# Moving the second mixture's small tiles in SBUF and adding two gaps between its tile pools

## The chip, the cores and the metric

The kernel runs on one core of a Trainium2 chip. The metric is the device time of one execution in microseconds; the time before is the median of 3 runs, 1181.48 us (1179.54 to 1184.17).

## The reference

An attention layer with a recurrent memory feeds a soft mixture of experts, and its result feeds a second mixture in which every expert sees every token and the shares P are balanced by eight rounds of row and column sums:

```python
def _moe2_ref(x, w_gate, w1, w2):
    N, D, E, F = (2304, 512, 8, 1024)
    P = np.exp(x @ w_gate - (x @ w_gate).max())
    for _ in range(8):
        P /= P.sum(1, keepdims=True) + 1e-09
        P /= P.sum(0, keepdims=True) + 1e-09
        P *= N / E
    out = np.zeros((N, D), dtype=np.float32)
    for e in range(E):
        h = np.maximum(x @ w1[e], 0.0)
        out += P[:, e:e + 1] * (h @ w2[e])
    return out
```

All inputs and outputs are float32.

## The kernel before, in words

The attention and the first mixture fill the first part of the program. The change touches only the second mixture, which works on 8 experts e times 9 units u of 256 tokens (72 units g in that order).

For each unit, `layer1` (L1030) makes the hidden layer: 8 matmuls `l`, each with a 128x128 piece of `a4s[e]` as the stationary operand and 256 columns of `c4T` as the moving one. ScalarE, VectorE and GpSimd (`hidden`, L1079) turn that into the tiles a11, a12, a22, s1, s2, s3, s4, each split into a high part h and a low part l of 2048 bytes per partition (four 128x128 stationary pieces); a21 of the first units shares its tile with s3. The second layer is a seven-product scheme: `product` (L1344) runs the products in the order p5, p1, p7, p6, p2, p3, p4, which pairs s1 with T1, a11 with B11, s3 with T3, s2 with T2, a12 with B21, s4 with B22 and a22 with T4. One product is 12 matmuls: for each of four pieces f, h against the weights' h (L1354), h against l (L1355) and l against h (L1356). The h and l tiles are stationary, and 256 columns of the weight tile W are moving. B11 and T3 lie in `BB1`, and B21 and B22 in `BB2`. After the second product, `layer1` of the next unit is put in. The first 6 units use `plain` (L1316) instead, with 48 matmuls of 512 moving columns. `collect` (L1359) adds each product onto the accumulators in VectorE. The order of TensorE, VectorE, ScalarE and GpSimd is written out by hand in this part (L1410 on); what stands outside that block, the writing of `sel` (L972, L978) among it, is placed by the scheduler as its operands and its space come free.

Places in SBUF. A pool's tiles lie one after another in the order in which they are first asked for, each rounded up to 32 bytes (buffers of one tag lie together), and the pools mA, mB, mC, mD follow each other in the order in which they are opened. The pools reuse space of the first mixture; with `reuse_waits="tile"` the first writer of a tile waits for the last user of whatever lay in that tile's own space. The first bytes of the tiles, by 512, are:

| tiles | pool | bytes per partition | start by 512 |
|---|---|---|---|
| c4T (moving in `layer1`) | cst | 9728 | 416 |
| T1, T2 of even experts, BB1 | mA | 4096, 8192 each | 416 |
| accA, accB, accD | mB | 18432, 18432, 9216 | 416 |
| Pr | mB | 576 | 416 |
| soB/c4, ahi, alo, a11, a21/s3, a12, a22, ft | mB | multiples of 512 | 480 |
| rr, cs | mB | 72, 32 | 480, 64 |
| cP, chi, f (3 buffers), s1, s2, s4 | mB | multiples of 512 | 96 |
| T1, T2 of odd experts, raw, BB2, T4 | mC | multiples of 512 | 96 |
| sel, Cw, gsel, m1, m2 | mD | 2560, 2304, 160, 4, 4 | 96, 96, 352, 0, 32 |
| a4 (2 buffers, stationary in `layer1`) | mD | 4096 each | 64 |

The 512 bytes are the length of one stationary piece (128 float32). The steps f go by 512 bytes in the hidden tiles, by 1024 or 2048 in the weights, and by 1024 per unit in c4T, so one residue holds for every matmul of a pair. In mD, `sel` lies on the bytes on which the first mixture keeps both of its `hT` tiles (L820), which its last matmuls (L848) read.

At the start of the second mixture VectorE copies `soT` (L858), writes `sel` (L972 once, L978 three times), copies `soB` four times (L1120) and makes `alo` (L1003); TensorE multiplies `ahi` and `alo` with `sel` (L1017, L1018) into the first `a4`, from which the first `layer1` runs.

Of the kernel before, what the change touches and what calls it, by code (L numbers as in the profile page):

```python
# [8 lines left out]
F32 = mybir.dt.float32  # L9
BF16 = mybir.dt.bfloat16  # L10
F32R = mybir.dt.float32r
# [10 lines left out]
def infini_attention_soft_moe_sinkhorn_moe(  # L22
# [18 lines left out]
    E = moe2_w1.shape[0]  # L41
    FF = moe2_w1.shape[1] * moe2_w1.shape[4]
    NS = moe_phi.shape[2]
    SPE = NS // E
    P = 128
# [8 lines left out]
    NTT = N // P  # L54
# [706 lines left out]
    with bctx:  # L761
# [57 lines left out]
        for g in range(E // 4):  # L819
# [3 lines left out]
            for n in range(FF // 512):  # L823
# [3 lines left out]
                for c in range(KD):  # L827
                    for j in range(4):
                        e = SPE * (4 * g + j)
# [41 lines left out]

    mA = ctx.enter_context(tc.tile_pool(name="mA", bufs=1, reuse_waits="tile"))
    mB = ctx.enter_context(tc.tile_pool(name="mB", bufs=1, reuse_waits="tile"))
    mC = ctx.enter_context(tc.tile_pool(name="mC", bufs=1, reuse_waits="tile"))
    mD = ctx.enter_context(tc.tile_pool(name="mD", bufs=1, reuse_waits="tile"))
    ps_l = ctx.enter_context(tc.tile_pool(name="ps_l", bufs=1, space=PSUM, reuse_waits="tile"))
# [91 lines left out]
        )  # L968


    sel = mD.tile([P, 4, 160], F32R, name="sel")
    nc.vector.tensor_scalar(  # L972
        out=sel.rearrange("p j c -> p (j c)"), in0=ones[:, 0:1].to_broadcast([P, 640]),
# [2 lines left out]
    for r in (0, 2, 4):  # L976
# [1 line left out]
        nc.vector.tensor_copy(  # L978
            sel[:, :, 32 * r : 32 * r + 32], ident.rearrange("p (j s) -> p j s", j=4)
        )  # L980
    a2s, a4s, G = {}, {}, {}

    def aux(nm):
        return ps_a.tile([P, 512], F32, tag="a", name=nm)
# [13 lines left out]
    def split_a(e):  # L998
        pa = a2s[e]
        ahi = mB.tile([P, 256], F32R, tag="ahi", name="ahi")  # L1000
        nc.scalar.activation(out=ahi, in_=pa[:, 0:256], func=AF.Copy)
        alo = mB.tile([P, 256], F32R, tag="alo", name="alo")
        nc.vector.tensor_tensor(  # L1003
            out=alo, in0=pa[:, 0:256], in1=ahi.bitcast(F32), op=ALU.subtract
        )
        a2s[e] = ahi, alo
        a4s[e] = mD.tile([P, FF], F32R, tag="a4", name="a4", bufs=2)

    def spread_a(e, n):

# [97 lines left out]

    soR = soT.rearrange("p c (o s) -> p c o s", o=1)
    Pr = mB.tile([P, NTT, E], F32, name="Pr")  # L1110
    Cw = mD.tile([P, NTT, NS], F32, name="Cw")

    gsel = mD.tile([P, E + NS], F32R, name="gsel")
    m1 = mD.tile([P, 1], F32, name="m1")
    m2 = mD.tile([1, 1], F32, name="m2")

    def gate_slots():
        soB = G["soB"] = mB.tile([P, KD, 4, NS], F32, tag="c4", name="soB")
# [51 lines left out]
        nc.scalar.activation(out=Pr, in_=Pr, func=AF.Exp, bias=m1)  # L1170

    def balance_rows():
        rr = mB.tile([P, NTT], F32, tag="rr", name="rr")
        nc.vector.tensor_reduce(out=rr, in_=Pr, op=ALU.add, axis=AX.X)
        nc.vector.tensor_scalar_add(rr, rr, 1e-9)
        nc.vector.reciprocal(rr, rr)
        nc.vector.tensor_tensor(
            out=Pr, in0=Pr, in1=rr.rearrange("p (t o) -> p t o", o=1).to_broadcast([P, NTT, E]),
            op=ALU.mult,
        )  # L1180
        cs = G["cs"] = mB.tile([P, E], F32, tag="cs", name="cs")
        nc.vector.tensor_reduce(
            out=cs, in_=Pr.rearrange("p t e -> p e t"), op=ALU.add, axis=AX.X
        )
# [56 lines left out]
    for n in range(8):  # L1241
        beside(9 + 3 * n, balance_rows)
        beside(10 + 3 * n, sum_columns)
        beside(11 + 3 * n, balance_columns)
# [43 lines left out]
    for e in range(1, E):  # L1288
        v = NU * (e - 1)
        for i in range(5):  # L1290
            c_steps(v + 6 + i, e, 2 * i, min(2 * i + 2, NU))
        at(v, 0, load_w1, e, e % 2)
        at(v + 3 * (e == 1), 4, load_raw, e)
        at(v + 1, 3, prepare_a, e)
        at(v + 1, 4, split_a, e)
        for n in range(2):
            at(v + 1, 5 + 2 * n, spread_a, e, n)
            at(v + 1, 6 + 2 * n, store_a, e, n)
        for i in range(2):
            for n, nm in enumerate(("T1", "T2", "T4")):  # L1300

                s = 29 + 4 * (3 * i + n) if e == 1 else 7 * (v + 2 + 3 * i + n) + 1
                beside(s, w_sum, e, nm, i, "P")
                beside(s + 2 - (e == 1), w_hi, e, nm, i)
                beside(s + 3 - (e == 1), w_lo, e, nm, i, "P")
            at(v + 6 + i, 2, w_sum, e, "T3", i, "P")
        for nm, k in (("B11", 2), ("T3", 4), ("B21", 6), ("B22", 8)):
            for i in range(2):
                at(v + 8, k + i, w_hi, e, nm, i)
                at(v + 8, k + i + (nm[0] == "B" and nm[1] == "2"), w_lo, e, nm, i, "D" if nm == "B22" and i else "P")  # L1310
# [99 lines left out]
    with tc.manual_schedule(engines={E_.PE, E_.DVE, E_.Activation, E_.Pool}):  # L1410
# [4 lines left out]
        prepare_a(0)  # L1415
        gate_slots()
        split_a(0)
        spread_a(0, 0)
        spread_a(0, 1)
# [105 lines left out]
```

## Time and profile before

| what | value |
|---|---|
| median of 3 runs | 1181.48 us |
| the profiled execution's own time | 1182.51 us |
| its span | 1180.7 us |
| TensorE matmul busy | 1120.1 us, 95% |
| VectorE busy | 865.7 us, 73% |
| ScalarE busy | 656.3 us, 56% |
| GpSimd busy | 641.8 us, 54% |
| granted TensorE clock, mean | 0.986 |

The busy time of TensorE is that of overlapping matmuls: one stands in the trace for some 280 ns while the next begins some 115 ns after it. A pause shorter than that overlap is not seen as idle time; the distance from one start to the next shows it.

### The profile page before, as it was taken

The numbers are of one execution on the slowest core, as the hardware profiler recorded it, in microseconds if no ns is written. First come the engines' busy times: TensorE is split into PE (matmuls) and PEld (weight loads), VectorE is DVE, ScalarE is ACT, GpSimd is POOL, SyncE is SP. The second block draws the span as 40 slices with busy tenths as digits, with TensorE's granted clock in tenths as the row PEclk, the third lists the DMA queues.
The fourth block names the chain that finished last, engine by engine and source line by source line (L and its number), as shares of the span: only waits on it lengthen the run. The fifth ranks groups of instructions, "written<-read, shape, count | busy, mean of one in ns | idle before, by whom it ended". The sixth has DMA issues, their size and how long they took to land.

```text
span 1180.7 us, 24363 instructions
## 1 busy us (share of the span) xinstructions
PE 1120.1 (95%) x9247; PEld 1018.6 (86%) x9247; DVE 865.7 (73%) x1891; ACT 656.3 (56%) x1422; POOL 641.8 (54%) x585
## 2 busy tenths in 40 slices
PE   6899999979799999999999999999999999999998
PEld 4677777764287888999999999999999999999998
DVE  6888888874337566677778767777876777788886
ACT  6788888741233487546545644654564465456342
POOL 5433323200323297577677767767776776686443
PEclk9999999998989999999999999999999999999999
DMA  6677686249702004002100400210040031000111
GB/s 158 192 200 226 197 245 178 74 187 376 309 6 71 1 2 143 1 2 82 62 2 1 143 2 1 92 53 1 1 143 1 2 108 37 2 1 19 42 50 54
DMA packets 37412, 102.32 MB, mean 87 GB/s; under 512 B 6448, under 2 KB 13232, under 8 KB 33200
## 3 DMA queue, kind: packets, MB, share of 16 engines
q1 hardware_dynamic: 36864, 100.69, 26.5%
q8 instruction: 73, 1.20, 0.4%
q14 instruction: 43, 0.35, 0.1%
q10 hardware_dynamic: 432, 0.09, 0.0%
HBM read 96.04 MB, written 4.72 MB: 85 GB/s over the span
## 4 chain that ended last, share of the span: by engine, by line
PE 75%; DVE 11%; ACT 7%; DMA 3%; issue 2%; POOL 1%; SPq 0%; ACTq 0%; DVEq 0%; POOLq 0%
PE y L1356 16%; PE y L1354 16%; PE y L1355 16%; PE l L1035 6%; PE y L1321 5%; PE po L436 3%; PE pt L399 2%; ACT sm L360 2%; DMA wm<-in_moe_w_dram 1%; PE pa L992 1%; DVE sm L356 1%; PE pc L1221 1%; PE ph L830 1%; DVE f L1059 1%; DMA raw<-in_moe_w_dram 1%
## 5 line engine op out<-in xcount | busy, mean ns | idle before, releaser
L1059 DVE SCALAR_TENSOR_TENSOR f<-l,f 128x512 f32<-128x512 f32 x264 | 181.4, 687 | 56.6 <-ACT a11h L1065 44.4
L1076 POOL TENSOR_TENSOR s1l<-f,s1h 128x512 fp32r<-128x512 f32 x66 | 88.4, 1340 | 170.0 <-ACT s1h L1065 165.9
L1370 DVE TENSOR_TENSOR accA<-accA,y 128x512 f32<-128x512 f32 (+1 forms) x129 | 86.6, 671 | 57.1 <-PE y L1356 51.6
L1065 ACT ACTIVATE a12h<-l 128x512 fp32r<-128x512 f32 x72 | 43.1, 598 | 121.6 <-DVE f L1059 121.6
L1076 POOL TENSOR_TENSOR s4l<-f,s4h 128x512 fp32r<-128x512 f32 x66 | 86.0, 1303 | 39.9 <-ACT s4h L1065 39.8
L1370 DVE TENSOR_TENSOR accB<-accB,y 128x512 f32<-128x512 f32 x129 | 88.3, 684 | 13.7 <-PE y L1356 2.3
L1035 PE MATMUL l<-c4T,a 128*128 128x256 f32 x576 | 82.7, 286 | 9.2 <-DVE a22l L1072 8.3
L1076 POOL TENSOR_TENSOR s2l<-f,s2h 128x512 fp32r<-128x512 f32 x66 | 85.9, 1301 | 0.8 <-ACT s2h L1065 0.8
L1076 POOL TENSOR_TENSOR s3l<-f,s3h 128x512 fp32r<-128x512 f32 x66 | 86.0, 1303 | 0.3 <-ACT s3h L1065 0.3
L1035 PEld LDWEIGHTS l<-c4T,a 128*128 128x128 f32 x576 | 75.0, 190 | 12.4 <-DVE a22l L1072 10.8
L360 ACT ACTIVATE sm<-sm,mn 128x128 f32<-128x128 f32 (+3 forms) x128 | 71.1, 556 | 19.5 <-DVE mn L356 17.9
L965 POOL TENSOR_TENSOR BB1l<-raw,BB1h 128x512 fp32r<-128x512 f32 x32 | 41.0, 1293 | 68.9 <-ACT BB1h L959 68.9
L1354 PE MATMUL y<-T2h,s2h 128*128 128x256 f32 x264 | 76.9, 291 | 0.0
L1354 PE MATMUL y<-BB2h,a12h 128*128 128x256 f32 x264 | 75.0, 284 | 0.0
L1355 PE MATMUL y<-BB2l,s4h 128*128 128x256 f32 x264 | 74.6, 283 | 0.1
L1354 PE MATMUL y<-BB1h,a11h 128*128 128x256 f32 x264 | 73.4, 278 | 1.3 <-DVE accB L1370 1.3
L1356 PE MATMUL y<-T4h,a22l 128*128 128x256 f32 x264 | 74.6, 283 | 0.0
L1356 PE MATMUL y<-BB2h,a12l 128*128 128x256 f32 x264 | 74.5, 282 | 0.0
L1356 PE MATMUL y<-BB2h,s4l 128*128 128x256 f32 x264 | 74.5, 282 | 0.0
L1354 PE MATMUL y<-BB2h,s4h 128*128 128x256 f32 x264 | 74.5, 282 | 0.0
L1354 PE MATMUL y<-T4h,a22h 128*128 128x256 f32 x264 | 74.3, 281 | 0.0
L1356 PE MATMUL y<-T1h,s1l 128*128 128x256 f32 x264 | 74.1, 281 | 0.0
(313 smaller groups left out, 4219.0 us busy)
## 6 DMA issues: line engine op xcount, KB each, us to landing
wm<-in_moe_w_dram SPq DMA_DIRECT2D x32, 1024.0 KB, 7.7
w<-in_moe_w_dram SPq DMA_DIRECT2D x32, 512.0 KB, 4.4
raw<-in_moe_w_dram SPq DMA_DIRECT2D x32, 512.0 KB, 4.1
qd<-in_q_dram SPq DMA_DIRECT2D x30, 288.0 KB, 4.2
kd<-in_k_dram SPq DMA_DIRECT2D x30, 288.0 KB, 4.5
qp<-in_q_dram SPq DMA_DIRECT2D x16, 288.0 KB, 3.4
vt<-in_v_dram SPq DMA_DIRECT2D x16, 256.0 KB, 2.7
out_dram<-accB SPq DMA_DIRECT2D x18, 128.0 KB, 1.8
```

Of the source, the lines that this page charges most:

```text
L360: nc.scalar.activation(out=sm[:, 0:n], in_=sm[:, 0:n], func=AF.Exp, scale=-1.0, bias=mnc, accum_out=X.sums[:, i, h : h + 1],)
L436: nc.tensor.matmul(po[64 * h : 64 * h + 64, c0:w], X.vt[:, j, h, :], rhs, start=(j == 0), stop=(j == n - 1),)
L965: eng(g).tensor_tensor(out=w_tile(e, nm, "l")[:, h], in0=full(e, nm, i), in1=w_tile(e, nm, "h")[:, h].bitcast(F32), op=ALU.subtract,)
L1035: nc.tensor.matmul(ph[:, f, :], a4s[e][:, P * (KH * j + f) : P * (KH * j + f) + P], c4T[:, UT * u : UT * u + UT], start=True, stop=True,)
L1059: nc.vector.scalar_tensor_tensor(out=f_tile(g, nm), in0=ph(g, src), scalar=0.0, in1=b, op0=ALU.max, op1=op)
L1065: nc.scalar.activation(out=h_tile(g, nm, "h"), in_=ph(g, nm) if a else FU[g, nm], func=AF.Relu if a else AF.Copy)
L1076: nc.gpsimd.tensor_tensor(out=lo, in0=FU[g, nm], in1=hi, op=ALU.subtract)
L1321: nc.tensor.matmul(Y[g, i], X[g, f"a{i}{j}", "hhl"[n]][:, f, :], BB[j, "hlh"[n]][:, f].rearrange("p a c -> p (a c)"), start=j == 1 and f = ...
L1354: nc.tensor.matmul(o_, hh[:, f, :], wh[:, f, :], start=f == 0, stop=False)
L1355: nc.tensor.matmul(o_, hh[:, f, :], wl[:, f, :], start=False, stop=False)
L1356: nc.tensor.matmul(o_, hl[:, f, :], wh[:, f, :], start=False, stop=f == KH - 1)
L1370: nc.vector.tensor_tensor(out=acc, in0=acc, in1=y, op=ALU.add)
```

## The change

A new pool mS is opened between mB and mC. It holds a tile of 96 bytes that nothing uses, and then gsel, m1, m2 (from mD) and rr, cs (from mB). In mD a tile of 64 bytes that nothing uses comes first, then the two buffers of a4 and Cw, and `sel` last. No instruction is added, removed or given other operands; the tiles' places differ.

```diff
     mB = ctx.enter_context(tc.tile_pool(name="mB", bufs=1, reuse_waits="tile"))
+    mS = ctx.enter_context(tc.tile_pool(name="mS", bufs=1, reuse_waits="tile"))
+    mS.tile([P, 24], F32, name="gap")
     mC = ctx.enter_context(tc.tile_pool(name="mC", bufs=1, reuse_waits="tile"))
...
+    mD.tile([P, 16], F32, name="gap")
+    a4s = {0: mD.tile([P, FF], F32R, tag="a4", name="a4", bufs=2)}
+    Cw = mD.tile([P, NTT, NS], F32, name="Cw")
     sel = mD.tile([P, 4, 160], F32R, name="sel")
...
-    a2s, a4s, G = {}, {}, {}
+    a2s, G = {}, {}
...
-        a4s[e] = mD.tile([P, FF], F32R, tag="a4", name="a4", bufs=2)
+        if e:
+            a4s[e] = mD.tile([P, FF], F32R, tag="a4", name="a4", bufs=2)
...
-    Cw = mD.tile([P, NTT, NS], F32, name="Cw")
-
-    gsel = mD.tile([P, E + NS], F32R, name="gsel")
-    m1 = mD.tile([P, 1], F32, name="m1")
-    m2 = mD.tile([1, 1], F32, name="m2")
+    gsel = mS.tile([P, E + NS], F32R, name="gsel")
+    m1 = mS.tile([P, 1], F32, name="m1")
+    m2 = mS.tile([1, 1], F32, name="m2")
...
-        rr = mB.tile([P, NTT], F32, tag="rr", name="rr")
+        rr = mS.tile([P, NTT], F32, tag="rr", name="rr")
...
-        cs = G["cs"] = mB.tile([P, E], F32, tag="cs", name="cs")
+        cs = G["cs"] = mS.tile([P, E], F32, tag="cs", name="cs")
```

## Rows read from the trace of the kernel before

**Rows 1.** Windows view: busy us and (x instructions) per engine, granted clock, DMA.

```profile
416.00:493.00 77.00, 71.86 (x611) 69.30 (x610) 48.92 (x81) 55.39 (x118) 55.85 (x44) 1.00 0.16 56
493.00:1094.00 601.00, 599.10 (x5166) 593.39 (x5166) 460.40 (x760) 324.48 (x613) 427.65 (x336) 1.00 0.11 37
1094.00:1181.00 87.00, 79.35 (x658) 77.92 (x656) 67.31 (x106) 29.27 (x51) 33.53 (x27) 1.00 0.15 49
```

**Rows 2.** Waits of TensorE, 493 to 1094 us: total us, times, longest.

```profile
PE l L1035 <- DVE a22l L1072: 0.6, 1, 0.6
```

**Rows 3.** Timeline, TensorE, expert 4: start us, us; first matmul of each product.

```profile
811.37 0.28 PE L1354 MATMUL y<-T1h,s1h 128*128 128x256 f32 x1
...
812.78 0.28 PE L1354 MATMUL y<-BB1h,a11h 128*128 128x256 f32 x1
...
814.15 1.12 PE L1035 MATMUL l<-c4T,a 128*128 128x256 f32 x8
815.11 0.28 PE L1354 MATMUL y<-BB1h,s3h 128*128 128x256 f32 x1
...
816.49 0.28 PE L1354 MATMUL y<-T2h,s2h 128*128 128x256 f32 x1
...
817.85 0.28 PE L1354 MATMUL y<-BB2h,a12h 128*128 128x256 f32 x1
...
819.28 0.28 PE L1354 MATMUL y<-BB2h,s4h 128*128 128x256 f32 x1
...
820.71 0.28 PE L1354 MATMUL y<-T4h,a22h 128*128 128x256 f32 x1
...
822.14 0.28 PE L1354 MATMUL y<-T1h,s1h 128*128 128x256 f32 x1
```

**Rows 4.** The same of one unit of expert 3 (some products left out).

```profile
708.87 0.28 PE L1354 MATMUL y<-T1h,s1h 128*128 128x256 f32 x1
...
710.30 0.28 PE L1354 MATMUL y<-BB1h,a11h 128*128 128x256 f32 x1
...
714.02 0.28 PE L1354 MATMUL y<-T2h,s2h 128*128 128x256 f32 x1
...
719.74 0.28 PE L1354 MATMUL y<-T1h,s1h 128*128 128x256 f32 x1
```

**Rows 5.** Timeline, VectorE and TensorE, one unit: the last split and the next layer1.

```profile
801.39 0.69 DVE L1072 SCALAR_TENSOR_TENSOR a22l<-l,a22h 128x512 fp32r<-128x512 f32 x1 [0.17 <-ACT a22h L1065]
...
803.38 0.40 PE L1035 MATMUL l<-c4T,a 128*128 128x256 f32 x2
803.58 0.69 DVE L1370 TENSOR_TENSOR accA<-accA,y 128x512 f32<-128x512 f32 x1 [0.68 <-PE y L1356]
```

**Rows 6.** Chain that ended last, one unit of expert 7: start us, us, what.

```profile
1134.95 1.21 PE l L1035 x8
...
1140.42 0.70 DVE accA L1370
...
1146.57 1.23 PE l L1035 x8
```

**Rows 7.** Groups by line: 512-column matmuls of the first units; xcount | busy, mean ns.

```profile
L1321 PE MATMUL y<-BB1h,a21l 128*128 128x512 f32 x24 | 9.6, 399 | 0.0
L1321 PE MATMUL y<-BB2h,a22l 128*128 128x512 f32 x24 | 9.5, 396 | 0.0
```

**Rows 8.** Timeline, VectorE and GpSimd, start of the second mixture.

```profile
316.12 1.41 DVE L972 TENSOR_SCALAR sel<-ones 128x640 fp32r<-128x640 f32 x1
317.14 5.17 POOL L965 TENSOR_TENSOR BB2l<-raw,BB2h 128x512 fp32r<-128x512 f32 x4
317.45 1.29 DVE L1120 COPY soB<-soT 128x128 f32<-128x128 f32 x1
318.66 3.74 DVE L978 CAST sel<-ident 128x128 fp32r<-128x128 f32 x3
...
323.81 0.41 DVE L1003 TENSOR_TENSOR alo<-pa,ahi 128x256 fp32r<-128x256 f32 x1
```

## The prediction, made before the changed kernel ran

> **What bounds the kernel now.** I read the windows view first, to find where TensorE is the bound and where it is not. From 493 to 1094 us TensorE is busy for 599.1 of 601 us at a granted clock of 1.00, and VectorE, the next, for 460 us [rows 1]. The waits of TensorE confirm it: in that stretch `layer1` waits once, for 0.6 us [rows 2]. Before it (416 to 493) and behind it (from 1094) 5 and 8 us are missing, so there other engines end some of the waits [rows 1]. From 493 to 1094 lie 53 units: 26 of the odd experts 1, 3, 5 and 7, and 27 of 2, 4 and 6.
>
> In a stretch where matmuls follow each other without idle time, the only thing left to gain is the distance between their starts, and busy time can't show that. So I went to the timeline of single units and subtracted the first starts of neighbouring products [rows 3, 4]. A product is 12 matmuls of the same shape; the reader is to see that they don't cost the same. With expert 4: s1 on T1 takes 1.41 us (117.5 ns a matmul), a11 on BB1 1.37 (114), s3 on BB1 1.38 (115), s2 on T2 1.36 (113), a12 on BB2 1.43 (119), s4 on BB2 1.43 and a22 on T4 1.43; the 8 of `layer1` take 0.96 (120 ns) [rows 3]. With expert 3, s1 on T1 takes 1.43 and the whole unit 10.87 us against 10.77 [rows 3, 4]. Line, shape and neighbours are the same for both experts; T1 and T2 alone lie elsewhere (mA for even, mC for odd experts).
>
> Set beside the table of places, as stationary start minus moving start by 512 bytes: a11 and s3 on BB1 are at +64 (480 - 416) and take 1.37 to 1.38 us; s1 and s2 of even experts are at +192 and take 1.41 and 1.36; `layer1` is at +160; a12 and a22 are at 384 and s4 at 0, with 1.43; s1 of odd experts is at 0, with 1.43. The two products at +64 are fast with every expert I looked at; no other distance is always fast.
>
> **The change part by part.** *Where the tiles go.* mB loses rr and cs in its middle (96 + 32 bytes after rounding), so f, s1, s2 and s4 move from 96 to 480, where a11, a12, a22 and s3 stay. mB then ends at 480. mS is 96 + 160 + 32 + 32 + 96 + 32 = 448 bytes, so mC begins at 416, as mA does. mD begins at 416 too; behind its gap of 64, a4 stands at 480 against c4T at 416. So all seven products and `layer1` are at +64, with even and odd experts.
>
> *Price of a matmul at +64.* Fast products of the rows cost 113 to 115 ns a matmul [rows 3]. Where a stream is settled, inside the product of a11, twelve take 1.37 us with the step over to `layer1`; s2 behind s3 takes 1.36 us, that is 113.3 ns. The first matmuls behind `layer1` (s3: 1.38) cost some 20 ns more, but they come out of a stream at +160, which will be at +64 as well. I take 113.3 ns and 4 ns per product for the steps: 7 x 1.364 + 8 x 0.1133 = 10.45 us for a unit. Against 10.77 that is 0.32 us, against 10.87 0.42 us [rows 3, 4]. The upper bound of the price is that every product costs 1.38 us as s3 does now: 10.57, a gain of 0.20 and 0.30.
>
> *The bound stretch.* 27 x 0.32 + 26 x 0.42 = 19.6 us. The low bound is 27 x 0.20 + 26 x 0.30 = 13.2, less a little where the four transposes of some units break the stream, so 13; the high one, with nothing for the steps (0.03 a unit more), 21. What could be late next is VectorE: it ends a22l at 802.1 us, and `layer1`, which needs the banks a22l reads, starts at 803.38 [rows 5], so 1.3 us are free; half a unit's gain is 0.2. It also still waits 0.68 us for TensorE at accA [rows 5], so it follows TensorE and not the other way round. I take the full gain.
>
> *The ends.* From 1094 us on each unit closes a ring through VectorE: `layer1` begins at 1134.95, TensorE ends p2 at 1140.42, and then VectorE and ScalarE work until the next `layer1` at 1146.57 [rows 6]. Only the first 5.5 us get faster: 8 x 6.5 ns and 36 matmuls by some 4.5 ns, 0.2 us for each of 6 rings, and about 0.7 us for the last twelve products, which have no ring: 2.0 us (1 to 3). From 416 to 493 us, 7 units wait in part for VectorE and ScalarE; of their 2.6 us at full price I take 1.0 (0 to 2.6). In the first 6 units the 512-column matmuls show no gain at +64: on BB1 399 ns a piece, on BB2 at 384 396 ns [rows 7]. Their 144 on BB2 go to +64, at 3 ns each a loss of 0.4 us, and `layer1` there gains 0.3: zero.
>
> *Start of the second mixture.* `sel` leaves the bytes of the first mixture's `hT`, and lies at the top, on tiles that the first mixture no longer uses in its second half. Now its four writes run from 316.12 us, between `soT` and `alo`; they take 1.41 and 3.74 us there, for each runs beside a subtraction of GpSimd of some 1.3 us and takes about as long [rows 8]. `sel` can then be written in a pause of VectorE ahead of 314 us. What stays ahead of `alo` are the four copies of `soB`. At the 1.29 us of the first they need 5.2 us and `alo` starts at 321.3; at the 0.5 us of the last three (which fill the time from the end of the last `sel` write at 322.4 to `alo` at 323.8 [rows 8]) it starts at 318.3, about where `ahi` ends. That is a gain of 2.5 to 5.5 us; if the scheduler leaves `sel` where it is, nothing. I take 3.0, as the copies fall into the time of GpSimd's subtractions, near the first row. The tiles in mC move by 320 bytes; they still lie on the same pieces of the first mixture's weights, so the loads wait for the same matmuls, and I cost that at nothing. The gaps and the other small tiles cost no instruction.
>
> *Sum.* 19.6 + 2.0 + 1.0 + 0 + 3.0 = 25.6 us. The profiled execution took 1182.5 us (span 1180.7), which gives 1156.9; the median of the runs is 1.0 us lower, so 1155.9, say 1156.
>
> [...] The rows show one matmul at 113 and another of the same form at 120 ns, with the places as the only difference I find [rows 3, 4]. [...]
>
> **The rivals.** *Places don't matter.* Then a11 and s3 are quick for another reason (their partner BB1 itself, or what other engines do beside them), and only the start gains: 1178 to 1181 us. For it: only BB1 is ever the moving tile at +64, so tile and distance can't be told apart there. Against it: T1 moved to another pool changes s1 from 1.41 to 1.43 [rows 3, 4]. [...] Chance 0.08.
>
> *The gain is taken back by the other engines.* In units with copies for the next expert VectorE or ScalarE may have less than the 0.4 us that a unit would shrink by. If half of the units can't follow, 19.6 becomes 9.8 and the time 1166. Against it: 1.3 us free in the ring [rows 5] and one wait in 601 us [rows 2]. Chance 0.09.
>
> *A stream stays in its bad state (slower).* Distance is not all: s1 and s2 of expert 4 are both at +192 and take 1.41 and 1.36 us; the second enters from a quick product [rows 3]. So the pace depends also on how a stream begins. If it enters badly behind each `layer1` and at +64 nothing breaks that state, all seven products run at 1.44, the worst seen, and `layer1` at 0.96: 11.04 us a unit, 0.27 and 0.17 more than now, 11.7 us in all, or 1190 with the start. It decides at a mean product of 1.41 us. Against it: s3 enters from `layer1` at +160 and still takes 1.38 [rows 3]. Chance 0.04.
>
> *`sel` stays late*, with the rest as forecast: 1159. It is inside the forecast, which has 0.79.
>
> **How the numbers follow.** The forecast is 1156. The terms' bounds give 13 + 1 + 0 + 0 - 0.4 = 13.6 to 21 + 3 + 2.6 + 5.5 = 32 us, or 1149 to 1168; all low or all high together is unlikely, but the upper end has to take in half a gain (1166), so I give 1149 to 1168. What is left out is the case without effect and the slower one, 0.12, and a little of the rest. A measurement of this kernel can tell about 0.5% (6 us) from no change: faster 0.88, same 0.08, slower 0.04.
>
> **What would show it.** Right: in the timeline each of the seven products takes 1.36 to 1.38 us with odd and even experts alike, `layer1` 0.91, and a unit without transposes 10.4 to 10.5; busy times of VectorE and GpSimd don't change; the writes of `sel` stand ahead of 314 us and `alo` before 322. Wrong: s4 and a22 at 1.43 as before (places don't matter, or not by this distance); products at 1.36 but units at 10.8, with new waits of `layer1` for a22l (taken back); all products at 1.40 and more (bad state).

## The result, and the profile after

The changed kernel takes 1169.24 us (median of 4 runs, 1166.49 to 1174.16), the kernel before 1181.63 us: a ratio of 0.9899 (95% interval 0.986 to 0.9938). That is 12.4 us less, where 25.6 were forecast; the forecast of 1156 and its whole range (1149 to 1168) lie below. The profiled execution took 1174.16 us, with a span of 1172.4 against 1180.7.

Windows of the same three stretches as [rows 1], same columns:

```profile
416.00:493.00 77.00, 70.49 (x611) 67.92 (x610) 49.87 (x84) 54.51 (x116) 55.95 (x45) 1.00 0.17 56
493.00:1094.00 601.00, 595.35 (x5208) 588.16 (x5207) 474.99 (x766) 326.68 (x617) 429.79 (x336) 1.00 0.11 38
1094.00:1181.00 87.00, 71.58 (x601) 69.41 (x599) 61.69 (x96) 27.38 (x47) 30.53 (x24) 0.99 0.13 43
```

TensorE is still the bound of the middle stretch at a granted clock of 1.00, and gets 5208 matmuls done where there were 5166. The busy time can't tell why it isn't more. The starts of the products can. Timeline, TensorE, one unit without transposes of expert 3, which answers [rows 4]: start, duration, what.

```profile
704.25 0.28 PE L1361 MATMUL y<-T1h,s1h 128*128 128x256 f32 x1
...
705.66 0.28 PE L1361 MATMUL y<-BB1h,a11h 128*128 128x256 f32 x1
...
707.07 1.11 PE L1043 MATMUL l<-c4T,a 128*128 128x256 f32 x8
708.01 0.28 PE L1361 MATMUL y<-BB1h,s3h 128*128 128x256 f32 x1
...
709.43 0.28 PE L1361 MATMUL y<-T2h,s2h 128*128 128x256 f32 x1
...
715.08 0.28 PE L1361 MATMUL y<-T1h,s1h 128*128 128x256 f32 x1
```

The same of expert 4, which answers [rows 3]:

```profile
805.67 0.28 PE L1361 MATMUL y<-T1h,s1h 128*128 128x256 f32 x1
...
807.03 0.28 PE L1361 MATMUL y<-BB1h,a11h 128*128 128x256 f32 x1
...
808.39 1.07 PE L1043 MATMUL l<-c4T,a 128*128 128x256 f32 x8
809.30 0.28 PE L1361 MATMUL y<-BB1h,s3h 128*128 128x256 f32 x1
...
816.10 0.28 PE L1361 MATMUL y<-T1h,s1h 128*128 128x256 f32 x1
```

With expert 4 each product takes 1.36 us (113.3 ns a matmul) and the unit 10.43 us; 10.45 were forecast. With expert 3 each product takes 1.41 us (117.7 ns) and the unit 10.83 us, though all distances are the same +64. Within a unit without transposes all products go at one pace now; between the two paces there is nothing. In this trace experts 1 and 3 go at 117.7 in these units and experts 2, 4, 5 and 6 at 113.3.

From the starts of the units, the span adds up like this (before, after): up to the first product of unit 6 415.9 and 414.2; units 6 to 11 77.2 and 77.1; the 53 units from there on 603.4 and 597.5; the end 84.3 and 83.7. So the bound stretch gave 5.9 us of the 19.6 forecast. Some 3.8 us of what is missing is one event of this execution: unit 0 of expert 6 takes 15.28 us, where the other units 0 from there on take 11.09 to 11.19, and the unit behind it is 0.4 us shorter than its like. Timeline of VectorE, then GpSimd, around it:

```profile
962.41 4.11 DVE L1213 TENSOR_TENSOR cP<-Cw,Pr 128x128 f32<-128x128 f32 x1
```

```profile
962.62 1.28 POOL L1084 TENSOR_TENSOR s4l<-f,s4h 128x512 fp32r<-128x512 f32 x1
963.87 2.50 POOL L969 TENSOR_TENSOR BB2l<-raw,BB2h 128x512 fp32r<-128x512 f32 x2
```

The small product cP, whose median is 0.39 us in this trace, lasts until GpSimd's three subtractions are over (they end at 966.37, cP at 966.52), and TensorE waits for what comes of it. Waits of TensorE from 493 to 1094 us, as in [rows 2]:

```profile
PE pc L1228 <- DVE c L1223: 2.4, 1, 2.4
...
PE l L1043 <- DVE a22l L1080: 1.5, 4, 0.6
```

In the trace of before no cP takes over 1.19 us; in one later run (distance 0, below) a cP takes 3.98 us once, again beside three subtractions of GpSimd. In the trace of the change a cP of 128x128 takes 0.28 to 0.29 us where no GpSimd instruction stands beside it and 0.29 to 1.94 us where one does, this one apart (4.11 us); in the trace of before 0.28 to 0.29 and 0.30 to 1.19. So the long ones stand beside GpSimd, and by the times of the two fences this one ran over three GpSimd instructions; what holds it there isn't shown.

### The profile page after: what moved, and what is told of

It is laid out like the page before. It is cut to its first block, busy times and chain, and to the rows that moved or that the text cites. A ratio compares the mean times of both kernels' runs of the same rounds, so it can differ in the third digit from the quotient of the medians.

```text
span 1172.4 us, 24365 instructions
## 1 busy us (share of the span) xinstructions
PE 1107.8 (94%) x9247; PEld 1004.2 (86%) x9247; DVE 874.6 (75%) x1891; ACT 657.7 (56%) x1422; POOL 643.1 (55%) x585
## 4 chain that ended last, share of the span: by engine, by line
PE 74%; DVE 13%; ACT 7%; issue 3%; POOL 1%; DMA 0%; SPq 0%; ACTq 0%; DVEq 0%; POOLq 0%
PE y L1361 15%; PE y L1362 15%; PE y L1363 15%; PE l L1043 5%; PE y L1328 5%; PE po L436 3%; ACT sm L360 2%; PE ph L830 2%; PE pt L399 1%; PE pso L848 1%; DVE sm L356 1%; DVE f L1067 1%; PE pa L999 1%; PE pc L1228 1%; DVE accB L1262 1%
## 5 line engine op out<-in xcount | busy, mean ns | idle before, releaser
L1361 PE MATMUL y<-T2h,s2h 128*128 128x256 f32 x264 | 77.2, 292 | 0.0
L1362 PE MATMUL y<-T2l,s2h 128*128 128x256 f32 x264 | 74.1, 281 | 0.0
L1363 PE MATMUL y<-T2h,s2l 128*128 128x256 f32 x264 | 74.1, 281 | 0.0
L1363 PE MATMUL y<-BB1h,s3l 128*128 128x256 f32 x264 | 73.5, 279 | 0.1
L1362 PE MATMUL y<-BB2l,a12h 128*128 128x256 f32 x264 | 73.5, 279 | 0.0
```

The source lines that it names most:

```text
L1361: nc.tensor.matmul(o_, hh[:, f, :], wh[:, f, :], start=f == 0, stop=False)
L1362: nc.tensor.matmul(o_, hh[:, f, :], wl[:, f, :], start=False, stop=False)
L1363: nc.tensor.matmul(o_, hl[:, f, :], wh[:, f, :], start=False, stop=f == KH - 1)
```

## Experiments

Theory after the result: at +64 a stream of matmuls has two paces, takes one behind a break (the transposes `pc`, the 32 matmuls `pa`, the four `p`) and keeps it. Rivals: the pace belongs to the tiles' places, or to what other engines do beside them; or distance doesn't count at all.

**The same program again, twice.** No edit.

> The changed kernel once more. Lock theory: at +64 a stream of matmuls settles at one of two paces, 113.3 or 117.7 ns, chosen in the first matmuls behind a break (the transposes of c, the matmuls of pa and p) and kept to the next break, up to four units long. The same program meets the same breaks, so the units without transposes take 10.43 us with even experts and 10.84 with odd ones again. Place theory (rival): the odd experts' weight tiles lie in mC, and a place in mC is slow in itself; it expects the same 10.43 and 10.84, so this run doesn't tell them apart. The one VectorE instruction of 4.1 us (cP, normal 0.35) should not come again: 1166 to 1170 us.

> The changed kernel a third time, unaltered. Theory (at +64 two paces exist, and a stream draws one of them anew behind each break, differently in each execution): the median of five rounds is 1166 to 1174 again; in the trace the units without transposes last 10.43 or 10.84 us, expert by expert, nothing between, and the experts that last 10.84 are not the same as in both earlier traces (1 and 3 in the first, 1 in the second). Rival (the pace follows from what is fixed in the program: the places, or the work beside it): experts 1 and 3, or 1 alone, are slow again.

1170.16 us (0.9891, 0.9865 to 0.9916) and 1169.64 us (0.9891, 0.9867 to 0.9915). One unit of expert 3 in the first of the two, and of expert 2 in the second:

```profile
708.41 0.28 PE L1361 MATMUL y<-T1h,s1h 128*128 128x256 f32 x1
...
718.84 0.28 PE L1361 MATMUL y<-T1h,s1h 128*128 128x256 f32 x1
```

```profile
608.39 0.28 PE L1361 MATMUL y<-T1h,s1h 128*128 128x256 f32 x1
...
619.23 0.28 PE L1361 MATMUL y<-T1h,s1h 128*128 128x256 f32 x1
```

Expert 3 now takes 10.43 us, and expert 2, at 10.43 in both other traces, 10.84. Slow are experts 1 and 3 in the first trace, 1 alone in the second, 2 alone in the third. The first expectation had all odd experts slow again, by either theory, and missed; the second, that other experts would be slow, came true. Places and instructions are the same in all three, so neither the places nor the order of the work fixes the pace. The 53 units take 597.5, 590.6 and 590.8 us.

**The distance itself.** Gaps and small tiles shift all eight pairs to one other distance; sel and the small tiles move along. For 0:

```diff
-    mD.tile([P, 16], F32, name="gap")
...
-    Pr = mB.tile([P, NTT, E], F32, name="Pr")
+    Pr = mS.tile([P, NTT, E], F32, name="Pr")
```

and for 320 (cut; 96 to 256 alike, with other sizes, 32 with smaller gaps):

```diff
+    gsel = mB.tile([P, E + NS], F32R, name="gsel")
+    m1 = mB.tile([P, 1], F32, name="m1")
+    m2 = mB.tile([1, 1], F32, name="m2")
+    mB.tile([P, 24], F32, name="gap")
...
+    Pr = mS.tile([P, NTT, E], F32, name="Pr")
-    mD.tile([P, 16], F32, name="gap")
+    mD.tile([P, 80], F32, name="gap")
```

> The changed kernel with stationary and moving operands both at residue 416 (distance 0): Pr goes to the small tiles' pool and the gap ahead of a4 is left out. Lock theory and distance theory alike: every product at 0 settles at 120 ns as s4 and the odd experts' s1 did before, units without transposes take 7 x 1.44 + 0.96 = 11.04 us, and the whole is some 10 us slower than the kernel before (1190 to 1195). If places don't matter at all: 1169 to 1182 and products as in either kernel.

> As the last, with gaps of 32 bytes, so that all eight pairs stand at +32. [...] Distance theory (64 bytes is a threshold): as at 0, 120 ns, 1190 us.

> All seven products and layer1 at +96: the small tiles are shared out between the front of mB and the small tiles' pool, and the gap ahead of a4 is 96 bytes. Lock theory (a stream keeps the pace it falls into behind a break; the distance sets which paces exist): a short list of paces, each held through a whole stream of 400 matmuls; if 64 bytes is the least distance at which the quick pace of 113.3 ns exists, it exists here too, possibly alone: units without transposes 10.43 us, or 10.84 where a stream holds 117.7. Distance theory (only +64 is quick): 117 to 120 ns throughout, 10.9 to 11.0 us.

> The same at +128. Lock theory: 113.3 ns exists here too, with or without 117.7 beside it: units without transposes 10.43 or 10.84 us. Distance theory: 10.9 to 11.0 us.

> The same at +192. In the kernel before, s1 of even experts held 117.5 ns at +192 and s2, entering from a product at +64, 113.3. Lock theory: both paces exist, each held through whole streams, so units without transposes take 10.43 or 10.84 us, and the choice may differ from expert to expert. Distance theory: +192 has one pace, the mean of what before showed, 115 to 118 ns, 10.7 us in all units.

> The same at +256, the farthest that two places can be apart by 512. [...] Distance theory: as +384 before, 119 ns, 10.95 us.

> All eight pairs at +320, that is 64 + 256. The looks at 0 and 256 gave the same 120 ns, and 64 and 192 both gave 113.3 and 117.7, so the distance seems to count by 256 and not by 512. Theory (by 256): as +64: streams at 113.3 or 117.7 ns, units without transposes 10.43 or 10.84 us, the whole 1166 to 1182. Rival (by 512, and 0 and 256 agree by chance): some other pace, 117 to 119 ns, 10.8 to 10.95 us in every unit.

One execution each; the kernel before beside them 1180.8 to 1182.0 us. "Unit" is one without transposes, "mean" the mean distance of two starts within the products and `layer1` of the 53 units, steps over 130 ns left out. The time at 64 is that of the profiled execution, with the 4.11 us of cP in it:

| distance | time, us | unit, us | mean, ns |
|---|---|---|---|
| 0 | 1195.92 | 11.04 | 119.9 |
| 32 | 1186.10 | 10.88 | 118.3 |
| 64 (the change) | 1174.16 | 10.43 or 10.84 | 115.2 |
| 96 | 1180.33 | 10.80 | 117.4 |
| 128 | 1188.48 | 10.92 | 118.7 |
| 192 | 1179.51 | 10.84, single products 1.36 | 117.1 |
| 256 | 1194.84 | 11.04 | 119.9 |
| 320 | 1168.93 | 10.43 or 10.84 | 114.9 |

Nothing but places differs, and the time goes from 1169 to 1196 us: the rival without distance has fallen. The distance counts by 256 bytes, not by 512: 0 and 256 are alike to 0.1 ns, and 64 and 320 are alike, with the same two paces; 192, that is -64, has the same two, with 113.3 in few streams only. At the other distances every unit without transposes takes the same time. The expectations of the lock theory, 113.3 at 96 and 128 as well, missed; so did those of the distance theory, 10.9 us or more at 96 and a single pace at 192. In all eight kernels the moving tiles start at 416, so this table alone doesn't tell the distance from the place of the stationary tile; the kernel before does: there s4 stands at 96 on a BB2 at 96, distance 0, and takes 1.43 us, 119 ns a matmul [rows 3].

**`layer1` at +160.** The places of a4 move by 96 bytes, and sel with them:

```diff
-    mD.tile([P, 16], F32, name="gap")
+    mD.tile([P, 40], F32, name="gap")
```

> The changed kernel with a gap of 160 instead of 64 bytes ahead of a4, so that layer1 alone stands at +160, as before the change, and the seven products stay at +64. Lock theory: each layer1 throws the stream out of its state, and in the kernel before the twelve matmuls behind it always came to 113 ns (120, 114, 123, 118, 113, ...); so units without transposes take some 10.50 us with odd and even experts alike (10.43 + 8 x 6 ns + 24 ns), odd ones gain 0.34, even ones lose 0.07, and the whole takes about 4 to 5 us less than the changed kernel. Place theory: odd experts stay at 10.84 plus 0.05, even ones go to 10.50, and the whole is 2 to 3 us slower than the changed kernel.

1169.96 us (0.9894, 0.9867 to 0.992). Timeline of one unit, `layer1` and the first product behind it:

```profile
704.97 1.12 PE L1043 MATMUL l<-c4T,a 128*128 128x256 f32 x8
705.92 0.28 PE L1361 MATMUL y<-BB1h,s3h 128*128 128x256 f32 x1
...
706.28 0.28 PE L1361 MATMUL y<-BB1h,s3h 128*128 128x256 f32 x1
...
706.63 0.28 PE L1361 MATMUL y<-BB1h,s3h 128*128 128x256 f32 x1
...
706.97 0.28 PE L1361 MATMUL y<-BB1h,s3h 128*128 128x256 f32 x1
```

`layer1` takes 0.95 us (119 ns a matmul), three matmuls behind it 0.36 and 0.35, then 0.34: 113.3 ns. Every unit without transposes takes 10.51 us, with all experts, and a stream that left `pc` at 117.7 changes to 113.3 behind the next `layer1`; at +64 it doesn't. (sel has moved too, so that the matmuls `p`, below, stand at 96 and 224 by 256; but between the transposes of units 7 and 8 and the next `layer1` there is no `p`.) So a short group at another distance can put a stream into the better pace. But 0.08 us a unit for that takes back what it gives: 592.1 us for the 53 units, and none of the 4 to 5 us that were expected of it.

**The transposes earlier.** A unit with transposes gains less than one without. If the wait for their operands were the reason, scaling and turning two steps earlier would help (with `layer1` at +160):

```diff
-        at(v, 1, scale_c, e, u0, u1)
-        at(v, 2, turn_c, e, u0, u1)
-        at(v, 3, store_c, e, u0, u1)
+        at(v, -1, scale_c, e, u0, u1)
+        at(v, 0, turn_c, e, u0, u1)
+        at(v, 1, store_c, e, u0, u1)
```

> layer1 at +160 and the products at +64, and the transposes of c one step list earlier: they stand behind the first product of a unit and not behind the third, so that layer1 follows a product later (scale_c and store_c move with them). Lock theory: the stream takes its chance behind the transposes, but only a11's twelve matmuls run at that pace; layer1 throws it out and everything behind it comes to 113.3. The units with transposes then take 10.95 us each, against 10.97 to 11.16 with layer1 at +160 alone: some 2.5 us less in all. Rival (a pause behind the transposes, not a pace, makes those units long): 11.0 to 11.2 as before, no gain.

1208.69 us (1.0223, 1.0195 to 1.0251): slower than before. Waits of TensorE, 493 to 1120 us:

```profile
PE pc L1228 <- DVE c L1223: 22.4, 24, 1.2
PE pc L1228 <- ACT c L1222: 10.2, 6, 3.8
```

Four kernels more followed: the same with sel on ScalarE (below), and three with `scale_c` at step -3, so that c is there in time (with +160, the same with sel on ScalarE, and at +64 with sel on ScalarE):

```diff
-        at(v, 1, scale_c, e, u0, u1)
-        at(v, 2, turn_c, e, u0, u1)
-        at(v, 3, store_c, e, u0, u1)
+        at(v, -3, scale_c, e, u0, u1)
+        at(v, 0, turn_c, e, u0, u1)
+        at(v, 1, store_c, e, u0, u1)
```

> Both edits together. The two don't touch the same stretch, so the gains add: 2.5 us from the units with transposes and 2.6 to 5 us from the start, 1162 to 1165 us, if layer1 at +160 alone is 1170.

> As l160_turn, but with scale_c four step lists ahead of the transposes (three before the unit's start) in place of one, so that TensorE doesn't stand still for c. Lock theory: only a11's matmuls run at the pace that the stream falls into behind the transposes, layer1 at +160 throws it out, and the units with transposes take 10.95 us (10.51 and the 0.44 of the transposes) in place of 10.97 to 11.16; the mean distance of the matmuls' starts goes from 115.1 ns to below 114.6, and the stretch of 53 units from 592 us to 588. Rival (what makes these units long is the pause around the transposes): the distance falls but the units stay at 11.0 to 11.2. If TensorE still waits for c, the units are longer by the waits.

> The same and the four writes of sel on ScalarE. The run with sel on ScalarE alone shortened the stretch from soT to the first matmul with sel from 8.1 to 5.7 us. The gains add: 2.4 us at the start and 3 to 4 us in the units with transposes against layer1 at +160 alone (1170), so 1163 to 1166 us.

> The control: layer1 at +64 as in the changed kernel, the transposes early and sel on ScalarE. Lock theory: with nothing at another distance a stream keeps the pace that it falls into behind the transposes for the whole unit, and the long streams behind p for four units, so the share of matmuls at 117 to 118 ns stays at that of the changed kernel (15 to 30 in 100) and differs from expert to expert; 1164 to 1170 us. Rival (the early place of the transposes alone makes the streams quick): as few slow matmuls as with layer1 at +160.

1206.04 (1.0193, 1.0161 to 1.0224), 1188.26 (1.004, 1.0021 to 1.0059), 1184.75 (1.002, 1.0004 to 1.0037) and 1190.31 us (1.0055, 1.003 to 1.0079). With +160 and step -3 the same view shows a part of where it went, 5.6 of the 18.9 us by which the 53 units are longer than with +160 alone (611.0 against 592.1):

```profile
PE y L1361 <- DVE accA L1377: 3.4, 10, 0.4
PE y L1362 <- POOL BB2l L969: 2.2, 6, 0.5
```

VectorE does the scaling ahead of the sums TensorE's banks wait for, and the units with transposes (those with `pa` left out) take 11.2 to 12.7 us instead of 10.97 to 11.16. In the last of the four, with `layer1` at +64, expert 4 goes at 10.83 again, so the early place of the transposes alone doesn't make the streams quick. The idea lost its own gain to new waits; that waits for c limit these units in the changed kernel isn't shown by it.

**sel on ScalarE.** The forecast of the start supposed that sel's four writes would leave VectorE's order between soT and alo. Timeline of VectorE in the changed kernel, which answers [rows 8]:

```profile
314.57 0.23 DVE L858 COPY soT<-psT 128x64 f32<-128x64 f32 x1 [0.81 <-PE psT L857]
314.71 1.23 DVE L979 TENSOR_SCALAR sel<-ones 128x640 fp32r<-128x640 f32 x1
315.86 1.29 DVE L1127 COPY soB<-soT 128x128 f32<-128x128 f32 x1
317.08 3.74 DVE L985 CAST sel<-ident 128x128 fp32r<-128x128 f32 x3
320.74 1.57 DVE L1127 COPY soB<-soT 128x128 f32<-128x128 f32 x3
322.23 0.41 DVE L1010 TENSOR_TENSOR alo<-pa,ahi 128x256 fp32r<-128x256 f32 x1
```

They didn't: from soT to alo 7.66 us, before 7.83 (soT starts at 315.98 there) [rows 8]; 7.03 and 7.22 in the two other traces of the changed kernel. The order of VectorE is the same, though sel no longer lies on the bytes of `hT`; what keeps it there isn't shown. So they were moved by hand (the write of zeros at L979 alike):

```diff
-        nc.vector.tensor_copy(
-            sel[:, :, 32 * r : 32 * r + 32], ident.rearrange("p (j s) -> p j s", j=4)
-        )
+        nc.scalar.activation(
+            out=sel[:, :, 32 * r : 32 * r + 32],
+            in_=ident.rearrange("p (j s) -> p j s", j=4), func=AF.Copy,
+        )
```

> The changed kernel with the four writes of sel on ScalarE in place of VectorE; nothing else. It measures the term of the start by itself: sel leaves VectorE's order between soT and alo. Theory (each copy of soB takes as long as the subtraction of GpSimd that it runs beside, 1.25 us): alo starts 5 us behind soT, and the stretch from soT to the first matmul with sel shrinks from 8.1 us (314.57 to 322.70) to some 5.5, 2.6 us less. Rival (the four copies are quick, 0.5 us each, once sel is gone): alo follows ahi, 2.6 us behind soT, and the stretch shrinks by 5 us. If something else holds the first matmul: no change.

1170.65 us (0.9893, 0.986 to 0.9926). alo starts 5.21 us behind soT:

```profile
315.74 0.22 DVE L858 COPY soT<-psT 128x64 f32<-128x64 f32 x1 [0.81 <-PE psT L857]
316.00 5.03 DVE L1128 COPY soB<-soT 128x128 f32<-128x128 f32 x4
320.95 0.41 DVE L1011 TENSOR_TENSOR alo<-pa,ahi 128x256 fp32r<-128x256 f32 x1
```

2.45 us earlier than in the first trace of the changed kernel: the four copies take 1.25 us each beside GpSimd. Unit 6 begins 98.7 us behind soT, against 99.6 there; but the two other traces of the changed kernel have 101.4 and 101.1 at this place, and the run with `layer1` at +160, with sel still on VectorE, has 98.0, and alo 5.90 us behind soT. Executions differ here by as much as the gain that is sought, so what the move is worth at unit 6 isn't shown; the median of the runs shows nothing.

**Both together.** +160 and sel on ScalarE.

> Two edits together: layer1 at +160 (which brought every stream behind it to the quick pace) and the four writes of sel on ScalarE (which brought alo forward by 2.4 us). Theory: units without transposes 10.51 us with all experts, alo some 5 us behind soT instead of 7.6, 53 units from 493 us on in 592 us as in the run with +160 alone; 1166 to 1169 us, that is 1 to 4 us under the changed kernel on the same chip. Rival (the earlier start only moves a wait, as the experiments with the transposes did): as with +160 alone, 1170.

1168.28 us (0.9874, 0.985 to 0.9898), 53 units in 591.5 us, 10.51 us a unit; within the scatter of +160 alone.

**What `p` does to a stream.** Behind the first product of unit 2 (the expectation below counts it to unit 1) stand four matmuls `p` (sel stationary, ahi and alo moving), and two products earlier four more. In the changed kernel their distances are 0 and 128 by 256. Timeline of the changed kernel, expert 3: the product s1 ahead, the first `p`, the product behind:

```profile
682.84 0.28 PE L1361 MATMUL y<-T1h,s1h 128*128 128x256 f32 x1
...
683.18 0.28 PE L1361 MATMUL y<-T1h,s1h 128*128 128x256 f32 x1
...
683.52 0.28 PE L1025 MATMUL p<-ahi,sel 128*128 128x256 f32 x1
...
684.34 0.28 PE L1361 MATMUL y<-BB1h,a11h 128*128 128x256 f32 x1
...
684.70 0.28 PE L1361 MATMUL y<-BB1h,a11h 128*128 128x256 f32 x1
```

The same place in the second trace of the same program:

```profile
687.72 0.28 PE L1361 MATMUL y<-T1h,s1h 128*128 128x256 f32 x1
...
688.08 0.28 PE L1361 MATMUL y<-T1h,s1h 128*128 128x256 f32 x1
...
689.60 0.28 PE L1361 MATMUL y<-BB1h,a11h 128*128 128x256 f32 x1
...
689.93 0.28 PE L1361 MATMUL y<-BB1h,a11h 128*128 128x256 f32 x1
```

From one row to the next are three matmuls. In the first trace the stream comes at 0.34 us for three and leaves at 0.36 (117.7 ns a matmul); in the second it comes at 0.36 and leaves at 0.33 to 0.34. In six traces `p` stands at 0 and 128: the three of the changed kernel, distance 320, sel on ScalarE, and the early transposes at +64. Each has twelve such groups from unit 10 on, and all 72 turn the pace over, 113 into 118 and 118 into 113. So `p` at these distances doesn't draw, it inverts; what differs from execution to execution is the pace behind `pa` ahead of it. The last experiment puts `p` at 32 and 160, with `layer1` left at +64, and sel's writes on ScalarE as above:

```diff
+    mD.tile([P, 40], F32, name="gap2")
     sel = mD.tile([P, 4, 160], F32R, name="sel")
```

> The changed kernel with the writes of sel on ScalarE, and 160 more bytes ahead of sel: the four matmuls p behind the first product of unit 1 then have their operands 32 and 160 bytes apart by 256 (the last of them 160) instead of 0 and 128; all else is as in the changed kernel, layer1 at +64 too. Theory A (a short group at 160 brings the stream behind it to the quick pace, as layer1 at +160 does in every unit of the earlier run): the units without transposes last 10.43 us with all experts, and the 53 units from 493 us on take 587 us (590.6 to 590.8 in the two better traces of the changed kernel, less one expert's 4 us); with 2.4 us from sel 1163 to 1166. Theory B (only the eight of layer1, or its own distance just ahead of the products, do that; four matmuls p leave the draw as it is): one to three experts at 10.84 again, 590 to 595 us, and 1166 to 1170.

1164.20 us (median of 5, 1162.16 to 1164.97), a ratio of 0.9842 (0.9829 to 0.9856): better than the change, by 5 us, and within 2.8 us from run to run, where the changed kernel scatters over 8 (1165.29 to 1173.43 in the six runs of its third measurement). The product behind `p`, expert 3:

```profile
681.26 0.28 PE L1363 MATMUL y<-BB1h,a11h 128*128 128x256 f32 x1
...
681.61 0.28 PE L1363 MATMUL y<-BB1h,a11h 128*128 128x256 f32 x1
...
681.95 0.28 PE L1363 MATMUL y<-BB1h,a11h 128*128 128x256 f32 x1
```

All twelve groups `p` leave at 113.3, nine that came at 113 and three that came at 118, and all units without transposes take 10.43 us with all experts: theory A of its expectation. The 53 units take 588.9 us, 2 more than expected, for the streams behind `pc` and `pa` keep their spread. Beside it stand 590.6 and 590.8 us in the traces with one slow expert, 593.7 in the one with two (less 3.8 for cP) and 594.5 with sel on ScalarE alone, where three are slow (1, 2 and 6): some 2 us for each slow expert. What else differs between these executions lies for the most part ahead of unit 6, and differs there between executions of the changed kernel too.

The start of this run shows what stands between alo and the units behind it. alo begins 4.21 us behind soT (314.58 to 318.79), 3.45 less than in the first trace of the changed kernel. Windows of that trace and then of this run; the granted clock is the third number from the end:

```profile
318.00:322.00 4.00, 0.00 (x0) 0.00 (x0) 4.00 (x5) 0.00 (x0) 3.96 (x4) 0.68 0.88 351
330.00:334.00 4.00, 4.00 (x19) 3.46 (x18) 2.33 (x6) 0.85 (x2) 0.00 (x0) 0.62 0.01 2
```

```profile
318.00:322.00 4.00, 1.90 (x9) 1.60 (x9) 1.89 (x3) 0.60 (x1) 4.00 (x4) 0.70 0.99 354
330.00:334.00 4.00, 4.00 (x13) 3.38 (x13) 0.26 (x1) 1.01 (x2) 1.42 (x2) 0.50 0.00 0
334.00:338.00 4.00, 4.00 (x17) 3.23 (x15) 0.33 (x2) 0.12 (x1) 1.16 (x1) 0.67 0.02 4
```

In both the granted clock falls from 1.00 to 0.50 at some 319.5 us, in the first while TensorE waits for alo, in this run 0.3 us behind the end of that wait. It is back at 1.00 from about 333 us on in the first, from 336.6 in this one (0.62 and 0.67 shared out between 0.50 and 1.00), 7.4 and 14.7 us behind the start of the first `layer1` (325.62 and 321.94), with no idle time of TensorE between. The work begins earlier and runs longer at a granted clock of 0.50, where the matmuls of 512 columns start 0.43 us apart instead of 0.23; the second `layer1` starts 24.6 us behind soT against 24.9, so of 3.45 us at alo 0.35 is left. That is one pair of traces, though. In the second and third trace of the changed kernel the clock rises 23.3 and 22.3 us behind soT (18.5 in the first, 22.1 in this run), and the second `layer1` starts 26.8 and 26.5 us behind it: beside those some 2 of 3 us are left. So the moment at which the clock rises moves by 4.8 us between executions of one program, more than alo was moved, and how much of an earlier alo the clock takes back isn't shown.

## Why the prediction was wrong

*The price of a matmul at +64: the step that failed.* 113.3 ns was the pace of s2 of expert 4, which stands at +192; a11 and s3, at +64, took 114 and 115 ns [rows 3]. It exists at +64 too, and for the streams that had it the price was right. What failed is that it was taken for the only one: the bounds (13 to 21 us) took the worst product seen at +64, 1.38 us, as the upper end. The same distance also allows 117.7 ns, 1.41 us a product, for up to 400 matmuls (four units) on end. The rows had a sign of it: s1 and s2 of expert 4, both at +192, took 1.41 and 1.36 us [rows 3], which are just these two paces. I made a rival of it ("a stream stays in its bad state"), and what it said of the mechanism came true for one or two experts in six; but I priced it for all experts and at 1.44, so it came out as a loss with a chance of 0.04, and not as a part of the likeliest case. By place in the expert, the 53 units add up to (us):

| units | before | forecast | after | second trace | p at 160 |
|---|---|---|---|---|---|
| 3 to 5 (18) | 194.7 | 188.0 | 190.1 | 188.9 | 187.7 |
| 2 and 6 (11) | 124.1 | 120.0 | 121.8 | 120.5 | 119.9 |
| 7 and 8 (12) | 135.3 | 130.9 | 132.7 | 132.5 | 132.1 |
| 0 (6) | 67.7 | 65.5 | 70.9 | 66.6 | 66.7 |
| 1 (6) | 81.6 | 79.4 | 82.0 | 82.0 | 82.5 |
| sum | 603.4 | 583.8 | 597.5 | 590.6 | 588.9 |

The forecast column takes 19.6 us evenly, 0.37 a unit. Where the pace is 113.3 throughout, units 2 to 6 reach the forecast (last column). Units 7, 8 and 0 give a little over half without the event above (3.9 of 6.6 us in the second trace), since each has transposes `pc` and a chance of the other pace behind them; and a unit 0 that comes in at 113.3 can stand still in s4: with expert 6 in the second trace s4 takes 1.58 us instead of 1.36, and its second matmul, which reads BB2l, starts at 970.42, when GpSimd's subtraction into BB2l has ended (970.36). Units 1 as a group give nothing in any trace: with experts 2 to 6 (6 in the first trace excepted) their a11 ends with a pause of 0.14 to 0.34 us ahead of `layer1`, which the kernel before doesn't have (1.50 to 1.70 us for the product instead of 1.36; 1.37 to 1.39 before); the one of expert 7 stands still in s1 and a11 before and after the change. What ends the pause is VectorE's a22l: with expert 6 in the second trace it ends at 976.14 and `layer1` starts at 976.20. The 1.3 us of VectorE that I counted as free were read in a unit without transposes [rows 5], and the one wait in 601 us that I set against this rival was two: the view of [rows 2] has a second line, 1.3 us for VectorE's accB. The rest of these units' gain I haven't taken apart. So here, and in some units 0, the rival "taken back" holds, in eight to ten units of a trace instead of half. Of the 6.8 us that the second trace lacks, 2.7 lie in units 1, 1.1 in units 0 and 3.0 in the others, where it is the pace. The 4.11 us of VectorE in unit 0 are the rest of the first trace's shortfall.

*The start: 3.0 forecast, none got.* The step said that sel can then be written in a pause of VectorE; that it can doesn't put it there. The low bound, nothing, was the right one. Where it was moved by hand, the copies took 1.25 us each in one run (near the 1.29 taken) and 1.0 in another; whether a gain at alo is one at unit 6 the traces don't settle (98.7 and 99.2 us behind soT, against 99.6, 101.4 and 101.1).

*The ends.* Rings of expert 7, 2.0 forecast: the chain of after has `layer1` at

```profile
1138.93 1.20 PE l L1043 x8
...
1150.56 1.21 PE l L1043 x8
```

that is 11.63 us, as before (11.62 [rows 6]); the whole end went from 84.3 to 83.7 us. Here the 0.2 us forecast for each ring don't show, and VectorE and ScalarE close the ring as before. Units 6 to 11, 1.0 forecast: 0.1. First six units, zero forecast: from soT to unit 6 99.9 and 99.6 us, right for this trace; the two others have 101.4 and 101.1, where the clock rises later (23.3 and 22.3 us behind soT instead of 18.5). The remaining 1.4 us of the first trace's gain lie in the first mixture, which ends (soT) at 314.6 instead of 316.0 us; in the two other traces it ends later than before, at 317.9 and 319.4.

*Places don't matter*: refuted by the distances, 113.3 to 119.9 ns for the same matmul at a granted clock of 1.00. The sign of the forecast and its reason, the distance, were right, though the reason is a distance by 256 bytes.

What stays open: what decides the pace behind `pc` and `pa`, and why a group inverts or sets it. All that is shown is which group does what.

## What to carry over

A measured best price of an instruction is a price only if everything that allows it is known: where the same row shows two values under the same conditions, price both and ask what holds each. In a dense stream of matmuls, subtract starts instead of reading busy time, choose the operands' distance by measurement, and look at the short groups between the streams: here 160 bytes ahead of the operand of the matmuls `p` kept the units without transposes at the quick pace with all experts, some 2 us for each expert that would have been slow (the kernel as a whole was 5 us quicker than the change, together with sel's writes on ScalarE, which alone gave nothing that could be measured). And before a wait is paid for with work moved earlier, follow the gain to the next point where another limit (a ring, a clock) sets the time.

## What the runs showed of the hardware that I had not expected

- The pace of back-to-back matmuls of 128x128 by 256 columns depends on the distance of their operands' first bytes by 256: 119.9 ns at 0, 118.3 at 32, 117.4 at 96, 118.7 at 128, and at 64 and 192 either 113.3 or 117.7.
- At 64 each pace holds for up to 400 matmuls. Four matmuls at 0 and 128 turn it into the other (72 of 72); four at 32 and 160 left 113.3 (12 of 12); behind the eight of `layer1` at 160 it was 113.3 in every unit without transposes.
- Within or just behind a wait of 2.5 to 6 us TensorE's granted clock fell from 1.00 to 0.50 and stood there until 333 to 342 us. Three executions of one program differ in it: the clock rose 18.5, 23.3 and 22.3 us behind soT; with the wait ended some 3 us earlier it rose 22.1 us behind it.
- A VectorE product of two small operands took 4.11 us beside three GpSimd subtractions, where the median is 0.39 and 0.28 to 0.29 us are taken with no GpSimd instruction beside it, and 3.98 once in another run (distance 0).
